# A recurrent-attention layer and a gated feed-forward layer in one kernel: another written-out order, with the loads of w first and unit 4's y transposed by a transfer

## The chip, the cores and the metric

The kernel runs on one core of one Trainium2 chip. The metric is the device time of one execution, in microseconds (us). The core has five engines that each run their own list of instructions in order and wait for each other by semaphores: TensorE (PE in the profile, its weight loads PEld) for matmuls, VectorE (DVE), ScalarE (ACT) and GpSimd (POOL) for elementwise work, and SyncE (SP), which only issues transfers. Transfers (DMA) are issued here from SP and from POOL.

## The reference

The first half is a linear attention with a decaying state, for each batch and head, over 768 tokens with head dimension 48. The second half multiplies two projections of its output and projects the product twice.

```python
def _attn_ref(r, k, v, w, u):
    B, H, S, D = r.shape                     # 4, 8, 768, 48
    state = np.zeros((B, H, D, D))
    for t in range(S):
        kt, vt, rt, wt = (k[:, :, t], v[:, :, t], r[:, :, t], w[:, :, t])
        cur = np.einsum('bhd,bhe->bhde', u[None] * kt, vt)
        y[:, :, t] = np.einsum('bhd,bhde->bhe', rt, state + cur)
        state = wt[:, :, :, None] * state + np.einsum('bhd,bhe->bhde', kt, vt)

def _moe_ref(x, w1, w2, w3, w_out):          # x: 3072 x 384, d_ff 1024
    a = x @ w1
    b = x @ w2
    h = a * b @ w3
    return h @ w_out
```

## The kernel before, in words

The tokens are cut into six chunks of 128, and the work into 13 units: a unit is one chunk of one or two batches (`UNITS`, line 14; units 0 and 1 are chunk 0 of one batch each, all others have two batches). For each unit t the following steps run; their names are those of the table `ORDER`.

*Loads* (lines 316 to 335): `win_t`, `kin_t`, `rin_t`, `vin_t`. Most are issued from POOL, where a transfer can change float32 to bfloat16. Unit 0's r, k and v come from SP as float32 and are cast by an engine (`rc_0`, `kc_0`, `vc_0`, line 330).

*Attention* (`unit`, from line 388): the logarithm of w (`ln`, line 408), its running sum over the chunk by a matmul with a triangle of ones LT (`cs`, line 424), the exponentials of it (`ne`, `e`), and k and r scaled by them (`KRk`, line 445, and `KRr`). k and r are needed transposed. TensorE does it by matmuls with an identity (`trk`, line 512, `trr`, line 497), with an eviction from PSUM behind (`trke`, line 516, `trre`); for the units in `DMA_K` and `DMA_R` a transposing transfer on SP's queue does it (`dtk`, `dtr`). The units in `RAW` transpose the unscaled r (`trw`, line 465), have the running sum a second time in transposed form (`csT`, line 453, its exponential `et`), and multiply afterwards (`KRw`, line 470). Then the scores of a chunk with itself (`m_t_b`, line 551) are masked in one VectorE step (`msk`, line 570) or, for the pairs in `POOL_MASK`, copied by ScalarE (`mcp`, line 557) and masked in place (`maff`, line 565 on POOL, line 563 on VectorE). y is summed in PSUM from the state (`ys`, line 586) and from the masked scores (`yi_t_b`, line 596); the diagonal term is formed beside (`rk`, `ruk`, `dg`, `dv`, lines 520 to 539), and `yb` (line 614) adds the two. `kv` (line 667, in the wide form of `KV_WIDE` line 660), `T`, `S` and `Sb` carry the state on to the next chunk.

*y transposed*: `yt` (line 633) on TensorE with the eviction `xT` (line 637), or, for the units in `DMA_Y`, two transposing transfers `dty_t_b` (line 623) on SP's queue.

*Feed-forward* (`block`, from line 698): groups `a_t_g` and `b_t_g` of x by w1 and w2 (line 714; two groups a unit in units 0 and 1, four otherwise), a's eviction `asb` (line 719), the product `abT` (line 724), then `o_t_b` (line 730), its eviction `osb` (line 735) and the store `st` (line 740). w3 times w_out is formed once: each of eight row blocks of w3 is transposed (`wt`, line 371, evicted by `w3Te`) and multiplied by w_out (`wm`, line 380, evicted by `w34e`). The weights come in pieces: w1 and w2 in halves (`w1_0`, `w1_1`, `w2_0`, `w2_1`; group g of a unit of two batches needs half 0 for g below 2), w3 in quarters (`w3_0` to `w3_3`), w_out whole (`wo`).

Nothing is scheduled by a program: `ORDER` (line 62) lists all steps with their engines, and each engine runs its steps in the order of that table. `warm7@5` in the table stands for five matmuls on zeros into bank 7 (line 308); they compute nothing that is used. `BANKS` (line 39) names the PSUM bank of each step and, in some keys, the buffer in SBUF (`M`: masked scores, `sa`: evicted a, `so`: output rows). The elementwise buffers of the attention steps exist twice, so unit t + 2 waits until unit t is done with them.

The lines that say where a step runs and when are these two, for the whole kernel:

```python
            name, _, eng = e.partition("@")
            steps[name](eng)
```

Of the kernel before, what the change touches and what calls it, by code (L numbers as in the profile page):

```python
# [56 lines left out]
sa10_2=1 a10_3=2 b10_3=2 sa10_3=0 o10_0=3 so10_0=3 o10_1=5 so10_1=2 cs11=0,1 m11_0=4,5 M11_0=2 m11_1=6,7 M11_1=3
y11=0,1 a11_0=2 b11_0=4 sa11_0=1 a11_1=1 b11_1=7 sa11_1=0 a11_2=6 b11_2=4 sa11_2=0 a11_3=0 b11_3=6 sa11_3=2 o11_0=7
so11_0=0 o11_1=2 so11_1=0 cs12=0,1 m12_0=2,3 M12_0=1 m12_1=4,5 M12_1=0 y12=0,1 a12_0=2 b12_0=1 sa12_0=0 a12_1=7
b12_1=6 sa12_1=2 a12_2=3 b12_2=0 sa12_2=0 a12_3=5 b12_3=4 sa12_3=1 o12_0=4 so12_0=3 o12_1=1 so12_1=1  # L60
# [3 lines left out]
mask1@DVE rin_2@POOL rin_0@SP rc_0@DVE warm0@13 cs_0@PE csT_0@PE ne_0@ACT win_1@POOL I128@POOL vin_2@POOL trw_0@PE  # L64
et_0@ACT kin_0@SP kc_0@DVE rk_0@DVE KRk_0@POOL warm6@5 trk_0@PE ln_2@ACT cs_2@PE pc_0@ACT trke_0@DVE KRw_0@DVE
m_0_0@PE w3_0@POOL u@SP uc@ACT mask@POOL rin_1@POOL vin_0@SP vc_0@ACT kv_0@PE ruk_0@DVE dg_0@DVE dv_0@POOL csT_2@PE
ne_2@ACT KRk_2@DVE trk_2@PE trw_2@PE S_0@DVE msk_0_0@DVE yi_0_0@PE kin_1@POOL rk_2@DVE et_2@ACT trke_2@ACT w1_1@POOL
ruk_2@POOL KRw_2@DVE yb_0@DVE warm5@3 m_2_0@PE m_2_1@PE mcp_2_1@ACT ln_1@ACT msk_2_0@DVE warm4@6 cs_1@PE yi_2_0@PE
dg_2@DVE csT_1@PE pc_1@ACT ne_1@ACT wt_0_0@PE wt_0_1@PE maff_2_1@DVE yt_0@PE xT_0@ACT yi_2_1@PE pc_2@ACT kv_2@PE
et_1@ACT dv_2@DVE KRk_1@DVE wt_1_0@PE trw_1@PE wt_1_1@PE yb_2@DVE yt_2@PE a_0_1@PE KRw_1@DVE trk_1@PE xT_2@ACT  # L70
trke_1@ACT a_2_3@PE S_2@DVE m_1_0@PE w3Te_1@ACT a_2_2@PE w1_0@POOL a_0_0@PE a_2_1@PE w2_1@POOL asb_2_2@ACT vin_1@POOL
# [62 lines left out]
def kernel(  # L134
# [254 lines left out]
    def unit(t):  # L389
# [151 lines left out]
        for b in range(nb):  # L541
# [248 lines left out]
```

## Time and profile before

| | |
|---|---|
| median of 3 executions | 168.65 us (168.05 to 200.98) |
| the profiled execution | 168.6 us, of it the span of the core's instructions 166.9 us |
| granted TensorE clock, mean | 0.990 |
| busy: PE / DVE / POOL / ACT | 154.8 / 129.7 / 106.7 / 96.9 us |
| matmuls on zeros (line 308) | 9.5 us |
| bytes moved | 25.63 MB, mean 154 GB/s |

The span runs from the first to the last instruction of the core; the time of the execution is 1.7 us longer. A busy share says how full an engine is on average; where the time goes is read from the stretches in which the engine that ends last has gaps. The time to landing of a transfer is counted from its issue, and so holds the wait behind the transfers ahead of it.

### The profile page before, as it was taken

What the parts mean: (1) busy time and instruction counts of PE and PEld (TensorE: products, weight loads), DVE (VectorE), ACT (ScalarE), POOL (GpSimd) and SP (SyncE); (2) the same over time, 40 slices, a digit from 0 to 9 for tenths busy, and PEclk for the clock granted to TensorE, in tenths of its full rate; (3) what the DMA queues carried; (4) which work ended last, traced back from release to release, by engine and by line L of the source; (5) the groups of instructions that cost most, each with busy time, mean ns of one, the idle gap of its engine ahead of it and who ended that gap; (6) DMA issues with size and microseconds to landing.
All of it is one profiled execution on the core that took longest, in us unless ns stands there. A gap on an engine that the chain in (4) does not pass through costs nothing.

```text
span 166.9 us, 4592 instructions
## 1 busy us (share of the span) xinstructions
PE 154.8 (93%) x1912; PEld 118.1 (71%) x1913; DVE 129.7 (78%) x203; ACT 96.9 (58%) x160; POOL 106.7 (64%) x96
## 2 busy tenths in 40 slices
PE   6866979999999999999899899997999999999991
PEld 2336568878677779678697677875779786988750
DVE  7339897667898899989998999898997986463610
ACT  3265456247976749995696768837582634252421
POOL 7987999266555099996939959995908770500000
PEclk9996999999999999999999999999999999999999
DMA  6999999999999959999999999999795999153033
GB/s 113 215 163 180 163 188 195 245 168 245 207 151 180 141 65 235 144 157 240 108 180 195 147 207 157 84 96 172 187 137 97 108 164 164 20 166 116 4 113 125
DMA packets 100789, 25.63 MB, mean 154 GB/s; under 512 B 92928, under 2 KB 98688, under 8 KB 100768
## 3 DMA queue, kind: packets, MB, share of 16 engines
q0 software_dynamic: 76208, 15.57, 106.9%
q1 hardware_dynamic: 24560, 9.77, 27.8%
q8 instruction: 15, 0.25, 0.7%
q14 instruction: 6, 0.05, 0.1%
HBM read 27.98 MB, written 4.72 MB: 196 GB/s over the span
## 4 chain that ended last, share of the span: by engine, by line
PE 74%; DVE 13%; DMA 5%; issue 4%; ACT 3%; POOL 1%; DVEq 0%; ACTq 0%; POOLq 0%
PE banks L714 31%; PE banks L730 16%; PE banks L380 6%; DMA win<-in_w_dram 5%; PE banks L551 4%; DVE Mbf L570 3%; PE banks L596 2%; PE banks L371 2%; PE banks L512 2%; DVE dv L539 2%; PE banks L424 2%; DVE KR L445 2%; PE banks L667 2%; PE banks L633 1%; DVE yb L614 1%
## 5 line engine op out<-in xcount | busy, mean ns | idle before, releaser
L714 PE MATMUL banks<-xT,w_bf 128*128 128x256 bf16 (+1 forms) x624 | 69.6, 264 | 1.7 <-DVE Mbf L570 1.7
L714 PEld LDWEIGHTS <-w_bf 128*128 128x128 bf16 x624 | 55.7, 98 | 9.4 <-issue 2.1
L719 ACT COPY a_sb<-banks 128x512 f32<-128x512 f32 x48 | 27.3, 590 | 25.8 <-PE banks L714 14.0
L724 DVE TENSOR_TENSOR abT<-a_sb,banks 128x512 bf16<-128x512 f32 x48 | 31.8, 681 | 8.6 <-PE banks L714 5.7
L730 PE MATMUL banks<-w,abT 128*128 128x384 bf16 x192 | 34.2, 326 | 0.0
L730 PEld LDWEIGHTS <-abT 128*128 128x128 bf16 x192 | 18.1, 98 | 10.7
L570 DVE TENSOR_TENSOR Mbf<-banks,mask 128x1024 bf16<-128x1024 f32 x14 | 17.1, 1218 | 4.3 <-PE banks L551 4.3
L735 ACT COPY osb<-banks 128x384 f32<-128x384 f32 x19 | 9.0, 480 | 14.1 <-PE banks L730 13.1
L614 DVE TENSOR_TENSOR yb<-banks,dv 128x768 bf16<-128x768 f32 (+1 forms) x13 | 11.6, 890 | 4.4 <-POOL dv L539 2.4
L335 POOL DMA_DIRECT2D win<-in_w_dram x12 | 13.9, 1158 | 1.4 <-POOLq L774 0.8
L408 ACT ACTIVATE lw<-win 128x768 bf16<-128x768 f32 (+1 forms) x13 | 10.4, 802 | 6.9 <-DMA win<-in_w_dram 6.9
L557 ACT CAST Mbf<-banks 128x1024 bf16<-128x1024 f32 x10 | 10.2, 1016 | 5.2 <-PE banks L551 3.7
L441 ACT ACTIVATE NEt<-banks 128x768 bf16<-128x768 f32 (+1 forms) x13 | 9.9, 761 | 4.2 <-PE banks L424 2.5
L565 POOL TENSOR_SCALAR_AFFINE_SELECT Mbf<-Mbf 128x1024 bf16<-128x1024 bf16 x5 | 5.4, 1102 | 10.5 <-ACT Mbf L557 10.5
L380 PE MATMUL banks<-wo_bf,w3T 128*128 128x384 bf16 x64 | 11.7, 326 | 0.0
L530 DVE TENSOR_REDUCE dg<-ruk 128x16 f32<-128x768 bf16 (+1 forms) x13 | 11.5, 885 | 0.1
L335 POOL DMA_DIRECT2D vin<-in_v_dram x8 | 9.1, 1140 | 3.8 <-DMA wo_bf<-in_moe_w_out_dram 3.2
L335 POOL DMA_DIRECT2D kin<-in_k_dram x8 | 9.1, 1142 | 3.0 <-PE banks L380 2.7
L335 POOL DMA_DIRECT2D rin<-in_r_dram x8 | 9.0, 1128 | 2.9 <-DMA w_bf<-in_moe_w_dram 2.2
L308 PE MATMUL banks<-zeros 128*128 128x512 bf16 x26 | 9.5, 525 | 1.5 <-DVE zeros L249 1.3
L486 POOL TENSOR_TENSOR KR<-rw,Et 128x768 bf16<-128x768 bf16 x3 | 4.9, 1639 | 8.5 <-DVE rw L478 5.4
L424 PE MATMUL banks<-lw,LT 128*128 128x384 bf16 x24 | 6.2, 325 | 2.7 <-ACT lw L408 1.8
(102 smaller groups left out, 257.2 us busy)
## 6 DMA issues: line engine op xcount, KB each, us to landing
out_dram<-osb SPq DMA_DIRECT2D x24, 192.0 KB, 2.3
win<-in_w_dram POOLq DMA_DIRECT2D x10, 384.0 KB, 8.6
w_bf<-in_moe_w_dram POOLq DMA_DIRECT2D x4, 512.0 KB, 13.3
w_bf<-in_moe_w_dram POOLq DMA_DIRECT2D x4, 384.0 KB, 6.9
kin<-in_k_dram POOLq DMA_DIRECT2D x7, 192.0 KB, 9.3
rin<-in_r_dram POOLq DMA_DIRECT2D x7, 192.0 KB, 9.5
vin<-in_v_dram POOLq DMA_DIRECT2D x7, 192.0 KB, 7.5
wo_bf<-in_moe_w_out_dram POOLq DMA_DIRECT2D x1, 768.0 KB, 10.6
```

The source lines that it names most:

```text
L335: QUEUE[eng].dma_start(dst, src)
L380: nc.tensor.matmul(one(f"wm{fi}")[:, :DM], lhsT=w3T[fi % 2][:, gi, :], rhs=wo_bf[:, gi, :], start=(gi == 0), stop=(gi == FI - 1))
L408: nc.scalar.activation(LW[:, :, :D], ww, Act.Ln)
L441: nc.scalar.activation(N_.rearrange("t (b h) d -> t b (h d)", b=nb), cs_view(), Act.Exp, scale=-1.0)
L530: nc.vector.reduce_sum(dgs, ruks, axis=AX.X)
L557: copier(eng)(Mbf[bank[f"M{t}_{b}"]], mview())
L570: nc.vector.tensor_mul(Mbf[bank[f"M{t}_{b}"]], mview(), mask.rearrange("s (j q) t -> s j q t", j=2))
L614: nc.vector.tensor_add(ybs.rearrange("t b (q e d) -> t e (b q) d", e=2, d=D), yview().rearrange("t e (x d) -> t e x d", d=D), dvs.rearrang ...
L714: nc.tensor.matmul(o[:, f, :], lhsT=wt[:, di, fi * P:(fi + 1) * P], rhs=x[:, di, :T], start=(di == 0), stop=(di == DI - 1))
L719: copier(eng)(a_sb[bank[f"sa{t}_{g}"]], one(f"a{t}_{g}"))
L724: nc.vector.tensor_mul(ab[:, g * per:(g + 1) * per, :T], sa.rearrange("p (f t) -> p f t", t=T), one(f"b{t}_{g}").rearrange("p (f t) -> p f ...
L730: nc.tensor.matmul(one(f"o{t}_{b}")[:, :DM], lhsT=ab[:, fi, b * C:(b + 1) * C], rhs=w34[:, fi, :], start=(fi == 0), stop=(fi == FI - 1))
```

## The change

Five tables change, no code. `DMA_Y` loses unit 8 and gains unit 4: y of unit 4 is now transposed by two transfers on SP's queue, and y of unit 8 by TensorE. `POOL_MASK` names ten pairs, five of them as before, `KV_WIDE` names units 3 and 4 in place of 1 and 10. `ORDER` and `BANKS` are new throughout; 71 steps change their engine, and every engine's list is in another order. There are 28 matmuls on zeros where the table had 27: 17 ahead of `cs_0` (13 before), then 5, 4 and 2.

```diff
-DMA_Y = {8, 9, 10, 11, 12}
+DMA_Y = {4, 9, 10, 11, 12}
 F32_IN = {0}
-POOL_MASK = {(2, 1), (3, 0), (5, 1), (6, 1), (7, 1), (8, 0), (8, 1), (10, 0), (11, 1), (12, 1)}
+POOL_MASK = {(2, 0), (5, 0), (6, 1), (7, 1), (9, 0), (10, 0), (10, 1), (11, 1), (12, 0), (12, 1)}
 Y_PE = set()
-KV_WIDE = {1, 10}
+KV_WIDE = {3, 4}
...
-table@ACT zeros@DVE padkr@DVE padet@DVE padlw@DVE win_0@POOL ln_0@ACT padr@DVE ones@DVE win_2@POOL kin_2@POOL LT@POOL
...
+table@ACT zeros@DVE kin_0@SP ones@DVE padlw@DVE kc_0@ACT win_0@POOL win_1@POOL padkr@DVE LT@POOL ln_0@ACT warm0@17
...
```

The built programs show what the tables make of it. First POOL's list at the start of the program, where the loads are issued; `win_0_78`, `win_1_79` and `win_2_80` are the w rows of units 0, 1 and 2, and so with kin, rin and vin. Before:

```order
L335 DMA win_0_78<-in_w_dram 128x8x48
L335 DMA win_2_80<-in_w_dram 128x16x48
L335 DMA kin_2_69<-in_k_dram 128x16x48
L259 ISA
L259 AFFINE_SELECT LT_148<-LT_148 128x128
L335 DMA rin_2_64<-in_r_dram 128x16x48
L335 DMA win_1_79<-in_w_dram 128x8x48
L263 AFFINE_SELECT I128_150<-I128_150 128x128
L335 DMA vin_2_74<-in_v_dram 128x16x48
L445 TENSOR_TENSOR KR_0_94<-kin_0_67,NEt_0_90 128x8x48
L361 DMA w3_bf_143<-in_moe_w3_dram 128x2x1024
```

And after:

```order
L335 DMA win_0_78<-in_w_dram 128x8x48
L335 DMA win_1_79<-in_w_dram 128x8x48
L259 ISA
L259 AFFINE_SELECT LT_148<-LT_148 128x128
L335 DMA win_2_80<-in_w_dram 128x16x48
L335 DMA kin_2_69<-in_k_dram 128x16x48
L263 AFFINE_SELECT I128_150<-I128_150 128x128
L335 DMA rin_2_64<-in_r_dram 128x16x48
L361 DMA w3_bf_143<-in_moe_w3_dram 128x2x1024
L335 DMA kin_1_68<-in_k_dram 128x8x48
L335 DMA rin_1_63<-in_r_dram 128x8x48
L335 DMA vin_2_74<-in_v_dram 128x16x48
```

The w rows of unit 1 move ahead of those of unit 2, the first quarter of w3 ahead of the v rows of unit 2, and unit 0's scaled k (`KRk_0`, line 445) leaves POOL. Behind these rows the weights now come as w2_0, w1_1, w2_1, w1_0, then the w rows of unit 3, then w_out; before they came as w1_1, w1_0, w2_1, w2_0, w_out, w rows of unit 3. The v rows of unit 3, which stood behind the last quarter of w3, stand ahead of the w rows of unit 4 and of that quarter.

Second VectorE's list between the masked scores of unit 0 and the first evictions of the feed-forward part; `Mbf_0_98` holds the masked scores of unit 0, and buffers with `_0_` in their name there are used by units 0 and 2, `_1_` by unit 1. Before:

```order
L570 TENSOR_TENSOR Mbf_0_98<-banks_61,mask_149 128x1024
L520 TENSOR_TENSOR rk_0_102<-rin_2_64,kin_2_69 128x768
L470 TENSOR_TENSOR KRT_0_96<-banks_61,ETt_0_92 128x1024
L614 TENSOR_TENSOR yb_0_110<-banks_61,dv_0_108 128x2x4x48
L570 TENSOR_TENSOR Mbf_2_100<-banks_61,mask_149 128x1024
L530 TENSOR_REDUCE dg_0_106<-ruk_0_104 128x16
L563 TENSOR_TENSOR Mbf_1_99<-Mbf_1_99,mask_149 128x1024
L539 TENSOR_TENSOR dv_0_108<-vin_2_74,dg_0_106 128x768
L445 TENSOR_TENSOR KR_1_95<-kin_1_68,NEt_1_91 128x8x48
L614 TENSOR_TENSOR yb_0_110<-banks_61,dv_0_108 128x2x8x48
```

And after:

```order
L570 TENSOR_TENSOR Mbf_0_98<-banks_61,mask_149 128x1024
L470 TENSOR_TENSOR KRT_0_96<-banks_61,ETt_0_92 128x1024
L520 TENSOR_TENSOR rk_0_102<-rin_2_64,kin_2_69 128x768
L445 TENSOR_TENSOR KR_1_95<-kin_1_68,NEt_1_91 128x8x48
L524 TENSOR_TENSOR ruk_0_104<-rk_0_102,u_bc_153 128x768
L530 TENSOR_REDUCE dg_0_106<-ruk_0_104 128x16
L614 TENSOR_TENSOR yb_0_110<-banks_61,dv_0_108 128x2x4x48
L570 TENSOR_TENSOR Mbf_2_100<-banks_61,mask_149 128x1024
L470 TENSOR_TENSOR KRT_1_97<-banks_61,ETt_1_93 128x512
L637 COPY xT_0_122<-banks_61 128x3x128
L614 TENSOR_TENSOR yb_0_110<-banks_61,dv_0_108 128x2x8x48
```

The sum of unit 2's y (the last row of both) now comes behind the eviction of unit 0's transposed y (`xT_0_122`, line 637), which ScalarE did; `ruk_2` comes from POOL, and unit 2's `dv` and the mask of its first scores (`maff_2_0`) go there.

In TensorE's list the feed-forward part opened with a_0_1, behind yt_2; it now opens with b_0_0, ahead of yt_2, with two matmuls on zeros right before it. `cs_1` and `csT_1` stand before unit 2's scores. The casts of unit 0's r and k go from VectorE to ScalarE, where that of r stands behind ln_1 and et_0; the cast of u goes from ScalarE to VectorE, that of v from ScalarE to POOL.

Third SP's list from the first output stores on; `osb` are output rows, `yb_0_110` is y of unit 4. Before:

```order
L740 DMA out_0_dram<-osb_2_139 128x384
L740 DMA out_0_dram<-osb_3_140 128x384
L335 DMA win_1_79<-in_w_dram 128x16x48
L740 DMA out_0_dram<-osb_2_139 128x384
L491 DMA_TRANSPOSE KRT_1_97<-KR_1_95 128x8x128
```

And after:

```order
L740 DMA out_0_dram<-osb_0_137 128x384
L740 DMA out_0_dram<-osb_2_139 128x384
L623 DMA_TRANSPOSE xT_0_122<-yb_0_110 128x3x128 x2
L491 DMA_TRANSPOSE KRT_1_97<-KR_1_95 128x8x128
L740 DMA out_0_dram<-osb_3_140 128x384
```

The two transposing transfers of unit 4 stand behind two stores and ahead of the transposed r of unit 7 (line 491); the w rows of unit 9 have left this queue for POOL's.

More of the change, by code (lines that the diff above doesn't have):

```diff
@@ L57 @@
[L57 to L60, printed above, removed]
+wt0=4 wm0=5 wt1=7 wm1=1 wt2=6 wm2=7 wt3=2 wm3=0 wt4=1 wm4=3 wt5=7 wm5=7 wt6=6 wm6=0 wt7=3 wm7=3 cs0=3 ct0=4 tr0=1
@@ L61 @@
 """
 ORDER = """
-table@ACT zeros@DVE padkr@DVE padet@DVE padlw@DVE win_0@POOL ln_0@ACT padr@DVE ones@DVE win_2@POOL kin_2@POOL LT@POOL
[L64 to L71, printed above, removed]
-b_2_3@PE w3Te_0@DVE msk_1_0@DVE rk_1@POOL yi_1_0@PE a_2_0@PE ruk_1@DVE dg_1@DVE dv_1@DVE Sb_2@DVE asb_2_3@ACT
@@ new lines @@
+KRk_0@DVE trw_0@PE w2_0@POOL trk_0@PE ln_2@ACT cs_2@PE KRw_0@DVE dg_0@DVE vin_0@SP pc_1@ACT pc_0@ACT trke_0@DVE
+vc_0@POOL kv_0@PE S_0@DVE ne_2@ACT KRk_2@DVE m_0_0@PE csT_2@PE et_2@ACT w1_1@POOL mask@POOL trk_2@PE dv_0@POOL
+msk_0_0@DVE trke_2@ACT trw_2@PE vin_1@POOL cs_1@PE ne_1@ACT KRw_2@DVE warm6@4 m_2_0@PE wt_1_0@PE pc_2@ACT w2_1@POOL
+wt_1_1@PE mcp_2_0@ACT rk_2@DVE w3Te_1@ACT w1_0@POOL yi_0_0@PE m_2_1@PE KRk_1@DVE trk_1@PE trke_1@ACT ruk_2@DVE
+dg_2@DVE yb_0@DVE kv_2@PE trw_1@PE msk_2_1@DVE wt_0_0@PE wt_0_1@PE maff_2_0@POOL yi_2_0@PE yt_0@PE KRw_1@DVE yi_2_1@PE
```

155 lines of the change are left out of this document (81 added, 74 removed).

## The prediction

> **What bounds the kernel now.** I read the busy time by stretch first, to see which engine is full and where it isn't. The columns are the stretch in us, then for PE, PEld, DVE, ACT and POOL the busy time and the number of instructions, then the granted TensorE clock, the DMA share and GB/s.
>
> ```profile
> 0.00:23.90 23.90, 18.13 (x174) 10.54 (x176) 16.54 (x36) 10.29 (x18) 21.27 (x27) 0.93 1.37 170
> 23.90:31.00 7.10, 6.89 (x96) 5.95 (x94) 5.28 (x10) 4.45 (x7) 5.91 (x7) 1.00 1.39 210
> 31.00:80.00 49.00, 49.00 (x705) 38.47 (x703) 43.05 (x69) 35.41 (x58) 32.84 (x28) 1.00 1.93 178
> 80.00:90.00 10.00, 9.28 (x93) 7.65 (x91) 9.08 (x13) 7.69 (x13) 7.09 (x7) 1.00 1.66 173
> 90.00:110.00 20.00, 19.45 (x299) 15.31 (x298) 19.47 (x29) 14.12 (x23) 17.85 (x13) 1.00 1.53 143
> 110.00:120.00 10.00, 8.89 (x100) 6.55 (x99) 8.98 (x11) 6.37 (x10) 8.10 (x8) 1.00 1.07 162
> 120.00:163.30 43.30, 43.18 (x460) 33.59 (x457) 27.28 (x41) 18.11 (x32) 13.63 (x12) 1.00 0.69 110
> ...
> sum 166.90, PE 154.81 PEld 118.05 DVE 129.69 ACT 96.89 POOL 106.68; mean PE 19.35 PEld 14.76 DVE 16.21 ACT 12.11 POOL 13.33
> ```
>
> From 23.9 us to its last matmul at 163.3 TensorE is busy but for 0.21 + 0.72 + 0.55 + 1.11 + 0.12 = 2.7 us. So the time is: when the dense work starts, plus that work, plus a tail of 166.9 - 163.3 = 3.6 us. The page's cost groups say what of the busy time is filler, the matmuls on zeros that keep the array running:
>
> ```profile
> L308 PE MATMUL banks<-zeros 128*128 128x512 bf16 x26 | 9.5, 525 | 1.5 <-DVE zeros L249 1.3
> ```
>
> Useful matmul time is 154.81 - 9.5 = 145.3 us, and the change keeps it: it trades y's transposes of unit 4 for those of unit 8 (same count), and the wide form of kv in units 1 and 10 for units 3 and 4. So what can be won is in the opening, where 23.9 us pass before the first matmuls of the feed-forward part (line 714), and in the 2.7 us of later idle. Third, I read the chain of waits through the opening (start us, us, what):
>
> ```profile
> 2.40 7.85 DMA win<-in_w_dram
> ...
> 10.33 0.84 ACT lw L408
> ...
> 11.24 0.40 ACT u_bc L304
> ...
> 12.79 1.23 DVE KR L445
> ...
> 14.07 1.03 PE banks L512 x8
> ...
> 16.50 1.06 PE banks L308 x2
> 17.55 0.57 PE banks L551 x16
> ...
> 22.39 0.96 DVE yb L614
> ...
> 23.39 0.51 PE banks L633 x6
> 23.90 0.67 PE banks L714 x12
> ...
> 25.60 0.35 PE banks L551 x8
> ...
> 40.05 0.45 PE banks L371 x8
> 40.50 0.45 PE banks L512 x8
> ```
>
> Everything hangs on unit 2: its w rows land at 10.25, its scores (m_2) start at 17.55, its y is added at 22.39 and transposed, and only then does the dense work begin, since a_0_1 stands behind yt_2 in TensorE's order.
>
> **The opening, step by step.** Loads: the w rows of unit 2 are now the third transfer of the GpSimd queue, behind those of units 0 and 1 and the making of LT.
>
> ```profile
> 1.34 2.24 POOL L335 DMA_DIRECT2D win<-in_w_dram  x2 [0.83 <-POOLq L774]
> ...
> 4.78 0.33 POOL L259 TENSOR_SCALAR_AFFINE_SELECT LT<-LT 128x128 bf16<-128x128 bf16 x1
> ```
>
> Two issues and LT take 1.34 + 2.24 + 0.33 = 3.91, against 2.40 now, and with the same 7.85 us to landing w arrives at 11.76, 1.5 us later. From landing to m_2_0 now takes 17.55 - 10.25 = 7.30 us. Out of this path go the cast of u on ScalarE (0.40) and the two matmuls on zeros (1.06) that stand right before m_2_0. The four zeros that replace them come earlier, while TensorE would wait for the eviction of unit 2's k. That gives 11.76 + 7.30 - 1.46 = 17.6. The long end keeps all of it: 19.06. The short end is a full clock for the two sets of eight transposes, of which one took 1.03 here against 0.45 later: 17.6 - 1.0, so 16.6 (the second set priced alike). I take 17.6, because the removals are rows of the chain and the clock is not known.
>
> From m_2 to the dense work: the first group is now b_0_0, which needs y of unit 0 only (and the first half of w2, issued among the first weights), and unit 2's y may come later. What lies ahead of it on VectorE after m_2 is, by like instructions, ruk_2, dg_2, yb_0, the mask of m_2_1, KRw_1 and xT_0:
>
> ```profile
> 16.68 0.55 DVE L614 TENSOR_TENSOR yb<-banks,dv 128x384 bf16<-128x384 f32 x1
> 17.93 1.23 DVE L570 TENSOR_TENSOR Mbf<-banks,mask 128x1024 bf16<-128x1024 f32 x1 [0.70 <-PE banks L551]
> 19.07 0.94 DVE L530 TENSOR_REDUCE dg<-ruk 128x16 f32<-128x768 bf16 x1
> ...
> 23.26 0.41 DVE L470 TENSOR_TENSOR KRT<-banks,ETt 128x512 bf16<-128x512 bf16 x1
> ...
> 30.79 0.36 DVE L637 COPY xT<-banks 128x384 bf16<-128x384 bf16 x1 [0.44 <-PE banks L633]
> ...
> 46.61 0.55 DVE L524 TENSOR_TENSOR ruk<-rk,u_bc 128x768 bf16<-128x768 bf16 x1
> ```
>
> Their sum is 0.55 + 0.94 + 0.55 + 1.23 + 0.41 + 0.36 = 4.04; with m_2's 0.57 ahead, xT_0 is ready at 17.6 + 0.57 + 4.04 = 22.2. TensorE's m_1_0 fits beside xT_0, and two matmuls on zeros follow (9.5 / 26 = 0.37 each): b_0_0 starts at 22.9.
>
> To compare, I count to a point where both kernels have done the same: all groups of units 0 to 2, cs_3, the first two products of w3 with w_out and the transposes of four w3 blocks. Now that is reached at 40.05 + 0.45 = 40.50, after 16.6 us with 0.21 idle, so 16.39 of work. The changed order does yt_2 (0.51) inside this stretch and has done m_1_0 (0.35) and trk_1 (half of a 0.45, 0.22) before it: 16.33. Started at 22.9 it ends at 39.2, a gain of 1.3 us. With m_2_0 at its short and long ends the gain is 2.3 and -0.2.
>
> It holds only if the weights keep up. The third piece of w3 (w3_2) is the tightest that I found:
>
> ```profile
> 27.19 0.74 POOL L361 DMA_DIRECT2D w_bf<-in_moe_w_dram  x1
> ```
>
> ```profile
> w_bf<-in_moe_w_dram POOLq DMA_DIRECT2D x1, 512.0 KB, 14.4
> ```
>
> ```profile
> 43.25 0.55 PE banks L371 x8
> ```
>
> Issued at 27.19, landed 14.4 us later at 41.6, used at 43.25: 1.65 us of cover. The same bytes stand ahead of it after the change, and GpSimd's queue issues the first four weight pieces without rk_1 and ruk_2 between them, so I don't let it land later; the cover is just enough for 1.3.
>
> **Unit 4's y.** Its six transposes and one eviction leave TensorE and ScalarE, two transposing transfers come onto SP's queue. The queue holds them behind two output stores, and dtr_7 behind them. The price is nothing if they land before a_4_0.
>
> ```profile
> L623 SPq DMA_TRANSPOSE xT<-yb x10: 1178/1240/1257, 108.6 to 146.4; - x10
> ```
>
> ```profile
> xT<-yb SPq DMA_TRANSPOSE x10, 2.5
> ```
>
> ```profile
> vin<-in_v_dram POOLq DMA_DIRECT2D x1, 192.0 KB, 13.2
> ```
>
> ```profile
> 58.15 2.71 PE banks L730 x16
> ...
> 61.18 1.31 PE banks L714 x12
> ```
>
> Between yi_4_1 and a_4_0 TensorE now has six groups of unit 3 (3 x 1.31), three outputs (1.5 x 2.71) and five sets of eight transposes or like (5 x 0.45): 10.2 us without its smaller steps. VectorE has five elementwise steps (0.55 each) and yb_4 (0.96) first: 3.7; the first issue takes 1.24 and the second transfer lands 2.5 after its own: 7.4 in all, 2.8 spare. The transfers of this row all lie after 108 us, with lighter loads. The nearest row for the loaded queue is the v load issued between 36 and 40 us, 13.2 to landing. I take 2.5, because that row has the same kind of transfer; the other end is a rival below.
>
> **The rest.** Steps of the later units change engines in both directions and masks change their form (14 on VectorE alone before and after); their waits are unknown. Bounds: the 0.72 + 0.55 + 1.11 = 2.4 us of idle between 80 and 120 us may vanish or double. I take no change. The last steps are again outputs of unit 12, an eviction and a store: the tail stays 3.6. The profiled execution took 168.6 us, 1.7 over its span, and the median is 168.65, so no correction is needed: 168.6 - 1.3 = 167.3 us.
>
> A row on contention belongs here:
>
> ```profile
> L539 DVE TENSOR_TENSOR dv<-vin,dg x5: 558/948/2395, 20.5 to 79.0; 128x768 bf16<-128x768 bf16 x4, 128x384 bf16<-128x384 bf16 x1
> ```
>
> The longest of these is dv_6, at 79.0, with GpSimd at work on KRk_7; it took 1.45 more than the median, and the idle 0.72 between 80 and 90 us came behind it. The change swaps the two engines of this pair and leaves GpSimd fewer elementwise steps. The Trainium skill (SBUF — State Buffer, Who interferes with whom) says that a VectorE instruction with two SBUF inputs contends with a GpSimd one that reads SBUF; by that the 0.72 goes, and the sum would be 166.6. I leave it out of the sum, because the row shows one such place and the new order makes others.
>
> **The rivals.**
> *Both gains at once (faster).* The opening at its short end, 2.3, and no idle from 80 to 120, 2.4: 168.6 - 4.7 = 163.9. For it: the idle places all lie where VectorE is busy 9.0 to 9.7 of 10, and dv_6, the longest step there, leaves VectorE. Against: as many steps move onto VectorE as off it, so it has no room to give.
> *The transfers bind.* TensorE reaches w3_2, w3_3 and unit 4's loads earlier, but v of unit 3 now goes ahead of the last piece of w3, and the loads land when they did: the gain is used up waiting, 168.6. For it: 1.65 of cover is little. Against: the bytes are the same.
> *The opening gets longer (slower).* Unit 0's casts move to ScalarE, r's behind ln_1 and et_0, so all of unit 0's products start later; w of unit 2 is 1.5 later. With m_2_0 at 19.06 the dense work starts 1.5 later than I say. If the array's clock is low there too, the products between 17 and 22 us (some 2 us of them at full clock, an estimate from x8 at 0.45 and m_2 at 0.57) take twice as long, 2 more: 167.3 + 3.5 = 170.8. For it: x8 transposes took 1.03 at 14.07, and 9 zeros now stand between cs_0 and the dense work's start where 14 stood (two more come at its edge). Against: TensorE's own steps are packed closer there. It decides from m_2_0 later than about 18.9. The Trainium skill (TensorE: Matmul & The Clock Gate, Part 1) says the array runs at half rate after an idle window of some 3.4 us until as long a busy one has passed; the row at 14.07 agrees in kind, though TensorE was not idle that long at a stretch. By that rule alone, with the idle no longer than now, the sum would stay 167.3.
> *y of unit 4 lands late (slower).* At 13.2 to landing it comes 3.7 + 1.24 + 13.2 = 18.1 after yi_4_1, against 10.2 of counted and up to 4 of uncounted work: 4 to 8 us of wait, 167.3 + 4 = 171.3 at its near end. It decides from a landing later than about 5.3 us.
> That the change doesn't do what it says is excluded by the built order.
>
> **Chances and range.** Forecast 0.50 (own range 166.2 to 168.4); both gains 0.13; transfers bind 0.14; longer opening 0.12; late y_4 0.06; other new waits in the middle, up to the doubled 2.4 (169.7), 0.05. What a measurement can tell here from no change is about 2%, 3.4 us: below 165.3 or above 172.0. Faster takes most of the both-gains case: 0.13 with the forecast's lower tail. Slower takes the far half of the two slower rivals and of the rest: 0.12. Same: 0.75. The range 164.6 to 171.0 takes in the forecast, the bound transfers, most of the longer opening and the near part of the fast case.
>
> **What would show it.** Right: the first matmul of line 714 at 22.9 (21.9 to 24.4), m_2 at about 17.6, no idle before the w3 transposes (line 371) between 39 and 46 us, transfers of y_4 landing within 5 us, TensorE idle 2 to 3 us from 31 us on. Wrong: a start past 24.2, idle at line 371 or 714 behind a transfer, or more than 4 us of new idle in the middle.

## The result, and the profile after

The changed kernel takes 170.12 us (median of 20 runs, 168.24 to 172.77), the kernel before 168.37 us (20 runs beside them): 1.0078 times as long, 95% interval 1.0051 to 1.0105. I had forecast 167.3 us and a small gain. The time lies in the range, and the change is within the 2% that I called no change, but the sign is wrong, and the interval shows that it is. The runs of the changed kernel differ among themselves by 2.7% (the twelve with a mean TensorE clock of 0.98 or less all took more than 169.3 us), and since a ratio leaves out every run more than 1.5% above the fastest of its kernel, the median over all runs stands beside it.

The profiled execution took 170.14 us, its span 168.4. Busy time by stretch, columns as in the prediction:

```profile
0.00:23.90 23.90, 19.81 (x213) 11.94 (x215) 15.06 (x38) 12.83 (x21) 22.03 (x29) 1.00 1.45 177
31.00:80.00 49.00, 49.00 (x676) 38.10 (x675) 42.70 (x64) 35.63 (x62) 36.85 (x30) 1.00 2.04 177
80.00:90.00 10.00, 9.86 (x147) 7.70 (x146) 8.88 (x15) 7.76 (x13) 8.29 (x7) 1.00 1.66 186
90.00:110.00 20.00, 18.80 (x226) 14.92 (x225) 18.43 (x27) 12.97 (x26) 11.04 (x10) 1.00 1.81 160
110.00:120.00 10.00, 8.66 (x130) 6.21 (x127) 9.97 (x15) 6.50 (x12) 4.53 (x3) 1.00 0.96 111
120.00:164.80 44.80, 42.90 (x440) 32.76 (x432) 30.39 (x40) 17.89 (x31) 12.12 (x9) 0.96 0.56 102
...
sum 168.40, PE 156.14 PEld 117.98 DVE 130.67 ACT 97.60 POOL 101.46; mean PE 19.52 PEld 14.75 DVE 16.33 ACT 12.20 POOL 12.68
```

The opening is shorter: TensorE works 19.81 of the first 23.9 us against 18.13, and from 31 to 80 us it does not stop. What was won there is lost behind 80 us. TensorE's idle from 80 us on is 0.14 + 1.20 + 1.34 + 1.90 = 4.6 us, against 2.5, and the last long stretch has a granted clock of 0.96 instead of 1.00. The clock makes the same work longer. The matmuls on zeros, to be taken off, are now:

```profile
L308 PE MATMUL banks<-zeros 128*128 128x512 bf16 x26 | 9.1, 510 | 1.5 <-DVE zeros L249 1.3
```

Without the zeros the matmuls take 156.1 - 9.1 = 147.0 us, 1.7 more than before, though they are the same matmuls but for the form of kv in four units.

The largest loss lies at 126 us. The first fence is VectorE's timeline there, the second GpSimd's, the third TensorE's (start us, busy us, line and operation, idle before and what ended it):

```profile
125.18 0.94 DVE L530 TENSOR_REDUCE dg<-ruk 128x16 f32<-128x768 bf16 x1
126.16 4.08 DVE L539 TENSOR_TENSOR dv<-wo_bf,dg 128x768 bf16<-128x768 bf16 x1
130.16 0.68 DVE L724 TENSOR_TENSOR abT<-a_sb,banks 128x512 bf16<-128x512 f32 x1
130.76 0.94 DVE L614 TENSOR_TENSOR yb<-banks,dv 128x768 bf16<-128x768 f32 x1
```

```profile
126.18 1.65 POOL L520 TENSOR_TENSOR rk<-rin,kin 128x768 bf16<-128x768 bf16 x1
127.78 1.64 POOL L520 TENSOR_TENSOR rk<-w_bf 128x768 bf16<-128x768 bf16 x1
129.50 2.25 POOL L524 TENSOR_TENSOR ruk<-rk,u_bc 128x768 bf16<-128x768 bf16 x1
```

```profile
128.69 1.46 PE L730 MATMUL banks<-w,abT 128*128 128x384 bf16 x8
131.76 0.40 PE L551 MATMUL banks<-KRT 64*128 64x128 bf16 x8 [1.60 <-DVE yb L614]
132.35 0.40 PE L551 MATMUL banks<-KRT 64*128 64x128 bf16 x8 [0.20 <-DVE abT L724]
```

dv_10 takes 4.08 us instead of 0.95 while GpSimd does rk_12, rk_11 and ruk_11 (lines 520 and 524) at its usual 1.65 and 1.64; ruk_11 is then 0.6 longer than the 1.65 it took before. Behind dv_10 stand abT of unit 9 and y of unit 10, and TensorE's next product, m_11_0, may not start before y of unit 10 has been read, since the new table of banks gives m11_0 the banks 0 and 1 that y10 holds. So TensorE waits 1.60 us. The bank table has a part in this wait, then, and no run here changes it alone. The same happens, shorter, at 114 us: rk_10 on VectorE beside rw_11 on GpSimd, and the out projection behind them waits 1.33.

```profile
114.17 2.35 DVE L520 TENSOR_TENSOR rk<-w_bf 128x768 bf16<-128x768 bf16 x1
114.44 1.65 POOL L478 TENSOR_TENSOR rw<-w_bf,iw 128x768 bf16<-128x768 bf16 x1
117.91 1.46 PE L730 MATMUL banks<-w,abT 128*128 128x384 bf16 x8 [1.33 <-DVE yb L614]
```

And after the idle at 130 us the clock falls, here by single microseconds:

```profile
130.00:131.00 1.00, 0.16 (x1) 0.09 (x1) 1.00 (x3) 0.07 (x1) 1.00 (x1) 1.00 1.70 151
131.00:132.00 1.00, 0.24 (x8) 0.24 (x8) 1.00 (x2) 0.51 (x1) 1.00 (x2) 1.00 1.31 243
132.00:133.00 1.00, 0.81 (x17) 0.54 (x12) 1.00 (x3) 0.21 (x1) 0.90 (x1) 1.00 0.04 8
133.00:134.00 1.00, 1.00 (x7) 0.61 (x6) 1.00 (x2) 0.80 (x1) 0.00 (x0) 0.63 0.61 100
134.00:135.00 1.00, 1.00 (x4) 0.44 (x3) 1.00 (x3) 0.00 (x0) 0.00 (x0) 0.50 1.68 83
135.00:136.00 1.00, 1.00 (x5) 0.46 (x4) 1.00 (x2) 0.00 (x0) 0.00 (x0) 0.50 2.03 159
136.00:137.00 1.00, 1.00 (x6) 0.53 (x5) 0.97 (x2) 0.48 (x1) 0.00 (x0) 0.66 0.80 50
```

Half the clock for 0.37/0.5 + 2 + 0.34/0.5 = 3.4 us costs 1.7 us of work.

Such long steps are not new. Among VectorE's products of two SBUF tensors of 128x768 from 31 us on, the kernel before has four above 1.1 us (2.40 at 79.0, 1.20 at 83.0, 1.59 at 98.4, 2.62 at 110.8), the changed one four as well (1.22 at 88.1, 1.32 at 96.4, 2.35 at 114.2, 4.08 at 126.2). Over their usual 0.55 and 0.95 that is 5.2 us lost before and 6.4 after: it is less the number of collisions that changed than where they stand and what waits behind them.

The account against before: the opening gives 40.50 - 37.71 = 2.8 us at the comparison point (worked out in the section on why), the idle takes 2.1 back and the clock 1.7. That leaves +1.0, and the span grew by 1.5; the other 0.5 I did not place.

### The profile page after: what moved, and what is told of

It reads as the page before. It is cut to its first block, busy times and chain, and to the rows that moved or that the text cites. A ratio compares the mean times of both kernels' runs of the same rounds, so it can differ in the third digit from the quotient of the medians.

```text
span 168.4 us, 4579 instructions
## 1 busy us (share of the span) xinstructions
PE 156.1 (93%) x1908; PEld 118.0 (70%) x1910; DVE 130.7 (78%) x204; ACT 97.6 (58%) x164; POOL 101.5 (60%) x92
## 4 chain that ended last, share of the span: by engine, by line
PE 69%; DMA 10%; DVE 7%; issue 5%; POOL 5%; ACT 1%; SPq 0%; POOLq 0%; DVEq 0%
PE banks L714 30%; PE banks L730 16%; PE banks L380 6%; DMA vin<-in_v_dram 5%; DMA KRT<-KR 5%; PE banks L551 3%; PE banks L596 2%; PE banks L371 2%; DVE abT L724 2%; PE banks L424 2%; PE banks L667 2%; POOL win L335 2%; PE banks L512 1%; PE banks L633 1%; PE banks L586 1%
## 5 line engine op out<-in xcount | busy, mean ns | idle before, releaser
L714 PEld LDWEIGHTS <-w_bf 128*128 128x128 bf16 x624 | 55.1, 98 | 7.9 <-issue 0.7
L730 PE MATMUL banks<-w,abT 128*128 128x384 bf16 x192 | 36.0, 337 | 1.3 <-DVE yb L614 1.3
L730 PEld LDWEIGHTS <-abT 128*128 128x128 bf16 x192 | 18.7, 100 | 13.3 <-issue 3.1
L565 POOL TENSOR_SCALAR_AFFINE_SELECT Mbf<-Mbf 128x1024 bf16<-128x1024 bf16 x6 | 6.9, 1145 | 16.7 <-ACT Mbf L557 15.8
L335 POOL DMA_DIRECT2D win<-in_w_dram x13 | 14.9, 1154 | 0.8 <-POOLq L774 0.8
L551 PE MATMUL banks<-KRT 64*128 64x128 bf16 x192 | 8.5, 217 | 2.9 <-DVE yb L614 1.6
L551 PEld LDWEIGHTS <-KRT 64*128 64x128 bf16 x192 | 5.7, 94 | 6.4 <-issue 4.4
```

Of the source, the lines that this page charges most:

```text
L335: QUEUE[eng].dma_start(dst, src)
L551: nc.tensor.matmul(o[:, e, q, :], lhsT=KRTs[a:a + PAD, 0, b * HP + q, :], rhs=KRTs[a:a + PAD, 1, b * HP + q, :], start=True, stop=True)
L714: nc.tensor.matmul(o[:, f, :], lhsT=wt[:, di, fi * P:(fi + 1) * P], rhs=x[:, di, :T], start=(di == 0), stop=(di == DI - 1))
L730: nc.tensor.matmul(one(f"o{t}_{b}")[:, :DM], lhsT=ab[:, fi, b * C:(b + 1) * C], rhs=w34[:, fi, :], start=(fi == 0), stop=(fi == FI - 1))
```

## Experiments

**My theory**: VectorE's steps that read two tensors from SBUF are held up by GpSimd's elementwise steps, the new order put them side by side at two places, and TensorE's clock falls after the longer of the two waits that follow. **The first rival**: TensorE would have waited for data in any case (transposed K and R, loads, y of unit 4), and the long VectorE steps only fill that wait. All kernels were timed beside the kernel before. TensorE's idle time by stretch is read from the same view as above (length of the stretch less the busy time):

| kernel | median us | ratio to before, 95% interval | idle 80-120 us | idle 120-140 us | clock 130-140 us |
|---|---|---|---|---|---|
| before | 168.4 to 168.7 | 1 | 2.38 | 0 | 1.00 |
| changed | 170.12 | 1.0078, 1.0051 to 1.0105 | 2.68 | 1.80 | 0.83 |
| rk_12, rk_11, ruk_11 off GpSimd | 168.54 | 1.0005, 0.9974 to 1.0036 | 3.02 | 0.94 | 1.00 |
| rw_11 off GpSimd | 168.57 | 0.9992, 0.9950 to 1.0033 | 0.55 | 1.79 | 0.83 |
| both | 166.76 | 0.9909, 0.9879 to 0.9940 | 1.60 | 0.94 | 1.00 |
| o_8_0 twice | 168.68 | 1.0037, 1.0001 to 1.0073 | 1.88 | 0.49 | 1.00 |
| y of unit 4 by TensorE | 169.94 | 1.0008, 0.9971 to 1.0046 | 2.55 | 1.79 | 0.83 |
| before, two products more on GpSimd | 176.63 | 1.0464, 1.0427 to 1.0502 | 2.38 | 6.37 | 0.83 |
| both, m_9 later | 167.18 | 0.9925, 0.9898 to 0.9952 | 1.65 | 0.94 | 1.00 |
| the same, rk_11 early | 165.90 | 0.9857, 0.9815 to 0.9899 | 1.66 | 0 | 1.00 |

The differences given below are between medians over all runs. By the ratios, the first four edits in the order of the table are 1.2, 1.45, 2.85 and 0.7 us faster than the changed kernel, and the interval of the fourth overlaps the changed kernel's. A third measure leaves out the opening, which differs from trace to trace: from the start of the out projection o_6_0 (109.69 us in the changed kernel's trace) to the end of the span it is 58.7 us in the changed kernel and 56.1, 57.4, 54.8 and 57.1 in the four, that is 2.6, 1.3, 3.9 and 1.6 less.

### One collision taken away, then the other, then both

```diff
-... rk_12@POOL ... rk_11@POOL ruk_11@POOL dg_11@DVE
+... rk_12@DVE ... rk_11@DVE ruk_11@DVE dg_11@DVE
```

> The changed kernel with three steps of VectorE's kind, rk_12, rk_11 and ruk_11, taken from GpSimd to VectorE at the same places of the list. Collision theory (in the changed kernel's trace dv_10 on VectorE took 4.08 us, not 0.95, while these three ran on GpSimd, and TensorE stood idle 1.60 + 0.20 us behind it and then ran 130-140 us at a granted clock of 0.83): dv_10 takes 0.95 us again, the 1.8 us of idle go, VectorE gets 3 x 0.55 = 1.65 us more work, a part of which may show; with the clock back the span falls by 1.8 + up to 1.7 us: 167 us, 166.5 to 168.5, ratio to the kernel before about 0.995. Late-data theory (TensorE would have waited for the transposed K and R or the loads in any case, the long dv_10 only filled the wait): the idle moves to another releaser and the time stays at 170.1, within 0.5 us.

Measured 168.54 us, 1.6 less than the changed kernel, and just past the long end (168.5) of what the collision theory gave. The clock is back, but 0.94 us of idle stay, for y of unit 11 behind VectorE's longer row. Only the three engine tags differ.

```diff
-cs_12@PE e_12@ACT rw_11@POOL yb_9@DVE
+cs_12@PE e_12@ACT rw_11@DVE yb_9@DVE
```

> The changed kernel with rw_11 alone taken from GpSimd to VectorE. Collision theory: rk_10 on VectorE, 2.35 us beside it in the changed kernel's trace, takes 0.55 us; yb_9 comes 1.3 us sooner and the 1.33 us of TensorE idle before the out projection at 117.9 us go; dv_10 keeps its 4 us unless the steps shift against each other. Time 170.1 - 1.3 = 168.8, 168.3 to 169.8, ratio about 1.002. Late-data theory: no change within 0.4 us, 169.7 to 170.5.

Measured 168.57 us, again 1.55 less. The idle from 110 to 120 us is gone (1.34 to 0), and dv_10, left as it was, still costs 1.79 us and the clock.

> Both edits at once: none of rk_12, rk_11, ruk_11, rw_11 on GpSimd. Collision theory: the gains add up, 3.1 us of idle and up to 1.7 us of lost clock: 165.5 to 167.5 us, ratio 0.985 to 0.995, so faster than both kernels, with the opening's gain of about 2.5 us kept. Late-data theory: 170 us within 0.6. Where VectorE becomes the bound instead (2.2 us more work on it from 110 to 140 us): 168 to 169.5.

Measured 166.76 us: 3.4 less than the changed kernel, about 1.6 + 1.55 added up (in the traces 2.6 + 1.3 = 3.9), and 0.9% faster than the kernel before. The late-data theory said 170 and falls. dv steps of the later units in this kernel, by the view of the tile:

```profile
L539 DVE TENSOR_TENSOR dv<-wo_bf,dg x3: 947/958/958, 105.1 to 136.5; 128x768 bf16<-128x768 bf16 x3
```

The longest is 958 ns, where it was 4,082. VectorE took over four steps at 0.55 us from GpSimd, 2.2 us, and lost the two long steps, 3.13 + 1.80 = 4.9 us: giving these steps to GpSimd had saved VectorE nothing.

### The clock by itself

```diff
-b_9_3@PE o_8_0@PE dty_10_0@SP
+b_9_3@PE o_8_0@PE o_8_0@PE dty_10_0@SP
```

> The changed kernel with the out projection of unit 8's first row issued twice (8 matmuls of 128x384 more, the same result written again), which fills 1.3 us of the 1.6 us in which TensorE stood idle at 130.2 us; dv_10 stays as long as it was. Clock theory (the granted clock falls to 0.83 after that idle because TensorE stood still): the clock of 130 to 140 us is back near 1.0 and the time falls by 1 to 1.7 us, 168.4 to 169.1, though more work is done. If the clock there has another cause: 130 to 140 us stay at about 0.83 and the time stays at 170.1, or rises by up to 0.3 us.

Measured 168.68 us, 1.4 less than the changed kernel with 1.3 us of matmuls more; by the ratios it is 0.7, not clear of noise, so the traces have to carry this part. dv_10 was as long as before, and y of unit 10 as late; only TensorE's idle was filled (its timeline, then the busy time of the stretch):

```profile
129.79 2.76 PE L730 MATMUL banks<-w,abT 128*128 128x384 bf16 x16
132.86 0.40 PE L551 MATMUL banks<-KRT 64*128 64x128 bf16 x8 [0.30 <-DVE yb L614]
133.45 0.40 PE L551 MATMUL banks<-KRT 64*128 64x128 bf16 x8 [0.19 <-DVE abT L724]
133.78 0.83 PE L714 MATMUL banks<-xT,w_bf 128*128 128x256 bf16 x6
134.45 2.76 PE L730 MATMUL banks<-w,abT 128*128 128x384 bf16 x16
```

```profile
130.00:140.00 10.00, 9.51 (x126) 5.99 (x124) 9.78 (x13) 3.47 (x5) 3.92 (x3) 1.00 1.08 121
```

The 16 matmuls of line 730 at 134.45 us take 2.76 us at the full clock; in the kernel with rw_11 off GpSimd, where the clock fell as in the changed one, they take 4.44:

```profile
132.45 4.44 PE L730 MATMUL banks<-w,abT 128*128 128x384 bf16 x16
```

The fall of the clock stands in the three traces with 1.8 us of idle at this place (the changed kernel, rw_11 off GpSimd, y of unit 4 by TensorE) and in none of those with 0.94 us or less. So it comes from TensorE standing still there, and it costs about as much as the wait itself: filling the idle gained 1.6 us behind o_6_0.

### The headline part: y of unit 4

```diff
-DMA_Y = {4, 9, 10, 11, 12}
+DMA_Y = {9, 10, 11, 12}
-yb_4@DVE dty_4_1@SP dty_4_0@SP
+yb_4@DVE ... yt_4@PE ... xT_4@ACT
```

> The changed kernel with its headline part undone: y of unit 4 goes through TensorE (12 matmuls of 128x128 more, 0.34 us) and ScalarE (one copy of 0.82 us) as it did in the kernel before, and its two transposing transfers fall away. Collision theory (the loss has nothing to do with y of unit 4): the two collisions late in the kernel stay, the time is 0.0 to 0.4 us above the changed kernel's, ratio 1.007 to 1.011. Late-data theory (the two transfers of y of unit 4 hold up the queue of transfers and with it what lands later): 1 us or more faster than the changed kernel, ratio 1.002 or less.

The ratio, 1.0008, would speak for the late-data theory and the median, 169.94, against it. I go by the trace (its execution took 170.73 us): both places of waiting stand in it unchanged (1.33 us from 110 to 120, 1.79 from 130 to 140, clock 0.83), and the idle of the other stretches from 31 us on is the changed kernel's within 0.15 us. So the transfers of unit 4 cause neither of the two waits. Whether they cost anything elsewhere, up to the 1.2 us between the two ratios, these runs do not tell.

### The collision alone, put into the kernel before

```diff
-kin_12@POOL m_10_1@PE
+kin_12@POOL rw_11@POOL rw_11@POOL m_10_1@PE
```

> The kernel BEFORE the change, with one thing added: GpSimd writes rw of unit 11 twice more (the same values), 2 x 1.64 us, in a stretch in which it stood idle, from about 122 us, while VectorE has rk_11 and dv_10, both with two inputs in SBUF, to do. Collision theory: one of these steps takes 3 to 4.5 us instead of 0.55 or 0.95, what follows on VectorE comes some 3.3 us later, of which 1.21 us are VectorE's idle time before abT at 127.7 us; TensorE gets an idle stretch of 0.5 to 2 us there and the time rises by 0.5 to 3 us (more where the clock falls): ratio 1.003 to 1.018. Rival (VectorE's long steps in the changed kernel waited for something else, GpSimd beside them is chance): rk_11 and dv_10 stay at 0.55 and 0.95 us and the time within 0.3 us.

Measured 176.63 us: 8 us more, far over the 3 that I gave at most. VectorE's and GpSimd's timelines, then TensorE's two waits:

```profile
122.52 1.99 DVE L520 TENSOR_TENSOR rk<-w_bf 128x768 bf16<-128x768 bf16 x1
124.43 2.39 DVE L539 TENSOR_TENSOR dv<-wo_bf,dg 128x768 bf16<-128x768 bf16 x1
...
128.22 5.16 DVE L486 TENSOR_TENSOR KR<-rw,Et 128x768 bf16<-128x768 bf16 x1
```

```profile
122.41 3.59 POOL L478 TENSOR_TENSOR rw<-w_bf,iw 128x768 bf16<-128x768 bf16 x2 [0.87 <-DVE KR L486]
...
128.94 1.65 POOL L524 TENSOR_TENSOR ruk<-rk,u_bc 128x768 bf16<-128x768 bf16 x1
130.55 0.83 POOL L689 TENSOR_TENSOR Sbf<-Tst,pc 128x384 bf16<-128x384 f32 x1
131.33 1.62 POOL L520 TENSOR_TENSOR rk<-rin,kin 128x768 bf16<-128x768 bf16 x1
```

```profile
127.59 2.78 PE L714 MATMUL banks<-xT,w_bf 128*128 128x256 bf16 x24 [2.37 <-DVE abT L724]
...
134.57 0.37 PE L596 MATMUL banks<-wo_bf,Mbf 128*128 128x48 bf16 x8 [4.00 <-DVE Mbf L570]
```

The two products held up rk_11 and dv_10 by 1.44 + 1.44 us: together what I expected, but spread over two steps, where I had one of them take 3 to 4.5 us. What I had not seen is what follows: VectorE, now 3 us late, reaches KRr_12 when GpSimd starts its row of ruk_11, the state and rk_12, and that one step lasts 5.16 us, until that row is over. In the kernel before, VectorE passes this place in time. One collision made the next. KRr_12 starts 0.72 us ahead of ruk_11, long enough for its usual 0.55, while GpSimd is issuing a load; what held it in that time is open. The kernel before has the same at 110.8 us: a step begun while GpSimd issues a load takes 2.62 us and ends 0.4 us behind the first GpSimd step that follows the load.

### What of GpSimd's work does it

The same place in the kernel before, with copies (one tensor read) and with memsets (nothing read) of a dead buffer in place of the products:

```diff
-kin_12@POOL m_10_1@PE
+kin_12@POOL copy@POOL copy@POOL copy@POOL m_10_1@PE
```

> The kernel BEFORE the change with three copies of r of unit 11 into the dead buffer of rw of unit 11 on GpSimd, at the place where the two extra products stood that made rk_11, dv_10 and KRr_12 long and the time 176.6 us. A copy reads one tensor in SBUF, the product two. If any step of GpSimd that reads SBUF holds up VectorE's steps with two inputs in SBUF: rk_11 and dv_10 together take the length of the copies longer, time 170 to 177 us. If only GpSimd's two-input steps do: rk_11 0.55, dv_10 0.95 us, time 168.6 within 0.5.

Measured 169.54 us, ratio 1.0068 (1.0043 to 1.0093), under the 170 that I gave for any step that reads: the two steps are 1.25 us longer together, not by the 3.48 us of the copies. With five memsets instead:

> The same place in the kernel BEFORE, with five memsets of the dead buffer of rw of unit 11 on GpSimd, which read nothing. If it is GpSimd's reading that holds VectorE up: rk_11 0.55 and dv_10 0.95 us, time 168.6 within 0.5 us. If any work of GpSimd on SBUF does, or the shift of GpSimd's later steps by some us is enough: rk_11 or dv_10 over 1.5 us, or the time 170 us or more.

Measured 168.74 us, ratio 1.0024 (1.0000 to 1.0047). GpSimd's and VectorE's timelines, first with the copies, then with the memsets (the added code moves dv from line 539 to 544):

```profile
122.02 3.48 POOL L531 COPY rw<-w_bf 128x768 bf16<-128x768 bf16 x3 [0.86 <-DVE KR L486]
122.14 1.18 DVE L520 TENSOR_TENSOR rk<-w_bf 128x768 bf16<-128x768 bf16 x1
123.24 1.57 DVE L544 TENSOR_TENSOR dv<-wo_bf,dg 128x768 bf16<-128x768 bf16 x1
```

```profile
122.40 4.07 POOL L531 MEMSET rw<- 128x768 bf16 x5 [0.69 <-DVE KR L486]
122.53 0.55 DVE L520 TENSOR_TENSOR rk<-w_bf 128x768 bf16<-128x768 bf16 x1
123.00 0.95 DVE L544 TENSOR_TENSOR dv<-wo_bf,dg 128x768 bf16<-128x768 bf16 x1
```

Beside 4.07 us of memsets the two steps keep their 0.55 and 0.95 us; beside copies each is 0.6 longer; beside products each is 1.44 longer. So it is GpSimd's reading of SBUF that holds VectorE up, and longer steps hold it longer. Of the two steps each is delayed by less than one GpSimd step beside it takes (1.64 us a product, 3.48 / 3 = 1.16 a copy). That reading counts and writing does not agrees with the Trainium skill (SBUF — State Buffer, Who interferes with whom), by which a VectorE instruction with two SBUF inputs contends with a GpSimd one that reads SBUF, not with one that only writes.

### Unit 9's late transfer, and VectorE's row before y of unit 11

In the changed kernel TensorE also waits 0.79 us at 107 us for a transposing transfer of unit 9. With both collisions gone it waited 1.05. The wait is not in every trace: with rw_11 off GpSimd and with o_8_0 twice, whose order up to there is the same, TensorE did not wait for it, and idle from 90 to 110 us was 0.55.

```diff
-b_7_3@PE m_9_1@PE ... m_9_0@PE b_7_2@PE ... yt_8@PE ... b_7_0@PE
+b_7_3@PE ... b_7_2@PE ... yt_8@PE ... b_7_0@PE m_9_1@PE m_9_0@PE
```

> The kernel with both groups of steps off GpSimd, and in addition the K R products of unit 9 (m_9_1, m_9_0) moved behind b_7_2, the transposes of y of unit 8 and b_7_0 on TensorE, that is 1.66 us of work later. In the trace of the kernel without this move the transposing transfer of unit 9's K landed 7.64 us after its issue and TensorE stood idle 1.05 us for it at 108.4 us. If that late landing is on the path that sets the end: 0.7 to 1.2 us faster than without the move, 165.5 to 166.1 us, ratio about 0.985. If VectorE's row of steps behind it is what counts (the products come later, so do mask and y of unit 9): no change, 166.4 to 167.1.

Measured 167.18 us, no gain over 166.76. The trace tells why, and I had not looked: cs_11 now stands right behind m_9_0 and writes the same banks 2 and 3, so TensorE waits for ScalarE's copy of m_9_0 instead.

```profile
110.11 0.48 PE L424 MATMUL banks<-lw,LT 128*128 128x384 bf16 x2 [1.11 <-ACT Mbf L557]
```

Next, VectorE's row at 131 to 138 us, behind which TensorE still stood idle 0.94 us:

```diff
-abT_9_3@DVE m_11_0@PE ... rk_12@DVE ... rk_11@DVE ruk_11@DVE ... ruk_12@DVE
+abT_9_3@DVE rk_11@DVE m_11_0@PE ... ruk_11@DVE ... rk_12@DVE ruk_12@DVE
```

> The kernel with m_9 later, and on VectorE rk_11 moved ahead of the mask of unit 11, into 0.78 us in which VectorE stood idle at 130.7 us, and rk_12 behind y of unit 11. In the trace without this, y of unit 11 came at 137.6 us at the end of an unbroken row of VectorE steps, and TensorE stood idle 0.94 us for it. If VectorE's row is what bounds there: y of unit 11 comes 0.9 us sooner and the time falls by 0.5 to 0.9 us against the kernel without this, ratio about 0.980. If TensorE finds a later wait instead: no change within 0.3 us.

Measured 165.90 us, 1.3 less than without it. From 120 to 140 us TensorE has no idle left. This is the fastest kernel of the study: 0.9857 (0.9815 to 0.9899) of the kernel before.

> The last kernel (both groups off GpSimd, m_9 later, rk_11 early) with the running sum of unit 11 (cs_11) moved behind the out projection o_6_0 on TensorE, 1.3 us later. In the traces with m_9 later TensorE no longer waits for the transposed K of unit 9, but 1.11 us for ScalarE's copy of m_9_0 out of the two banks that cs_11, right behind it, writes: the wait had only moved. If that wait is on the path: 0.7 to 1.1 us faster than the kernel without this, 164.8 to 165.3 us, ratio about 0.979. If another wait takes its place again: within 0.3 us of 165.9.

Here cs_11 goes behind o_6_0. The wait of 1.11 us is gone from the trace, three smaller ones (0.29, 0.16 and, behind the transposed y of a unit, 0.36 us) stand in it instead, and the time is not better: 166.2 us is the median of five of the six times (164.91 to 167.68; the sixth, 538 us, I leave out), ratio 0.9864 (0.9818 to 0.9910). The difference from the kernel without it is within what six runs can tell. Whether unit 9's transfer is worth anything stays open.

### The opening's order of weights

```diff
-vin_2 w2_0 w1_1 ... b_0_0@PE ... a_0_1@PE
+vin_2 w1_1 w2_0 ... a_0_1@PE ... b_0_0@PE
```

> The kernel with rk_11 early (both groups off GpSimd, m_9 later), with one part of the change's opening undone: the first half of w1 is loaded ahead of the first half of w2 again, and the first group of the dense work is a_0_1, as in the kernel before, instead of b_0_0. If the opening's gain comes from this order of the weights: the dense work's first group starts about 1 us later (24 us and more) and the time is 1 us longer, about 166.9. If it comes from the order of the w rows and of the first steps, which stay: the first group starts between 21.5 and 23.3 us as in the eight traces with the new opening, and the time stays at 165.9 within 0.6 us.

Measured 166.07 us (0.9842, 0.9810 to 0.9874), the same as the 165.90 without it. The first group starts at 23.69 us, 0.4 past the 23.3 that I gave; the trace without it has 23.24. So w2 ahead of w1 is not where the opening's gain comes from.

## Why the prediction was wrong, point by point

- **What bounds the kernel** (start, dense work, tail): right, and the tail is 168.4 - 164.8 = 3.6 us as forecast. That the useful matmul time stays at 145.3 us was wrong, 147.0, because I took the clock of the dense work as given.
- **The opening, gain 1.3 (2.3 to -0.2)**: right in mechanism and sign, too small. In the changed kernel's trace m_2 starts at 16.57 (forecast 17.6, short end 16.6) and the first matmul of line 714 at 21.47 (22.9):

```profile
16.57 0.40 PE L551 MATMUL banks<-KRT 64*128 64x128 bf16 x8
...
21.47 0.83 PE L714 MATMUL banks<-xT,w_bf 128*128 128x128 bf16 x12
```

  The comparison point, the end of the four w3 blocks' transposes, is reached at 38.16, and by then this order has done one set of eight (0.45) more than I counted: 37.71, against 40.50 before and 39.2 forecast. The chain of waits there:

```profile
37.94 0.22 PE banks L371 x4
38.16 0.45 PE banks L465 x8
```

  That is the early end of a spread. In nine traces with this opening m_2 starts between 16.6 and 18.5, mean 17.4, the dense work between 21.5 and 23.3, mean 22.3, and the point lies between 37.7 and 39.6, mean 38.7; in four with the old opening the point lies between 40.5 and 40.9, mean 40.7. So the gain is 2.0 us on average. The start of m_2 was well taken; the mis-sized terms are the way from it to the dense work (4.9 us, forecast 5.3, since VectorE's six steps overlap at their ends and take 3.8, not 4.04) and the single trace of before (40.5, at the early end). The rival of half clock in a longer opening did not come: the clock from 12 to 20 us was granted between 0.57 and 1.00 from trace to trace, and even at 0.57 the dense work starts at 23.2, earlier than before.
- **The loads**: right. No idle stands before line 371 or 714 from 31 to 80 us (49.00 of 49.00 busy). It is not so in every execution: in the trace with o_8_0 twice TensorE stops there for 0.47 us, at 53 us, behind the late landing of a load of w rows.
- **y of unit 4**: hidden, as forecast, but not by my number. The row of SP's timeline and, from the view of transfers between 61.5 and 64 us, the landing:

```profile
62.08 2.77 SPq L623 DMA_TRANSPOSE xT<-yb  x2
```

```profile
xT<-yb SPq DMA_TRANSPOSE x2, 7.6
```

  They land after 7.6 us, not 2.5: the row from the lightly loaded end of the kernel was the wrong one. a_4_0 does not wait because the smaller steps that I had not counted lie ahead of it as well, and y of unit 4 undone moved neither of the two large waits. I said that it decides from 5.3; that was too early.
- **"The rest ... I take no change"**: this is the step that failed. Its bounds, 0 to 4.8 us of idle between 80 and 120 us, held (2.68), and it was the wrong stretch: the largest new wait lies at 130 us, where the kernel before had none, and the clock's 1.7 us that follow a wait were in no term at all. Together the middle and late part cost about 170.12 - 168.37 + 2.0 = 3.75 us. That the time still lies in the stated range is luck: the room above 169.7 was left for a longer opening, which did not come, and the opening, 0.7 us better than forecast, took a part of the loss away.
- **The row on contention**: I had the cause in my hand. I wrote that the order swaps one such pair (dv_6 and KRk_7) and "makes others", and left it there. In the new order that pair no longer overlaps (KRk_7 on VectorE at 74.9 us takes 0.55, dv_6 on GpSimd at 77.5 takes 1.47), and the idle between 80 and 90 us fell from 0.72 to 0.14. That agrees with the Trainium skill's rule there (SBUF — State Buffer, Who interferes with whom), though no run changes this pair alone. The others could have been looked for in the built order, which does not show by itself that they overlap in time: dv_10 on VectorE with rk_12, rk_11 and ruk_11 in a row on GpSimd, rk_10 beside rw_11. Two collisions of the size of the row that I quoted (1.45 us each), on stretches where VectorE is 9 to 10 of 10 busy, would have made the sum 167.3 - 0.6 + 2.9 = 169.6 us.
- **The rivals**: "other new waits in the middle", 0.05, up to 169.7, is what came, a little past its 169.7, and it got the smallest chance. Late y of unit 4, bound transfers and a longer opening did not come. That what would show me wrong was "more than 4 us of new idle in the middle" set the mark too high: 2.1 us of new idle and the clock were enough.

What stays open: 0.5 us of the account; why the changed kernel's times spread over 2.7% (one execution of it was traced); what unit 9's transfer costs; what the new bank table costs.

## What to carry to other kernels

Where a scheduler moves elementwise steps between VectorE and GpSimd, list for the new order which VectorE steps that read two tensors from SBUF can fall beside GpSimd steps that read SBUF, and price each pair by the length of the GpSimd step, not by VectorE's own. A step on GpSimd that takes three times as long as on VectorE (1.64 against 0.55 us) relieves nothing when it stands beside such work; four tags changed back turned a loss of 0.8% into a gain of 0.9%. Where TensorE's idle is gathered in one place, the clock's fall can cost as much again as the wait (1.7 us behind 1.8).

## What I had not expected of the hardware

- A VectorE step can be passed over by several GpSimd steps in a row: dv_10 (0.95 us) took 4.08 us and ended 0.8 us behind the second of two of them, KRr_12 (0.55 us) took 5.16 us and ended 0.4 us behind the third of three.
- 1.8 us of idle between 130.1 and 132.4 us was followed, from 133.3 us on, by 3.4 us at half the clock. 1.1 us (at 114 us in the kernel before), 1.3 (at 118 us in the changed one), 0.5 (with o_8_0 twice) and even 2.4 in a row (at 125 us, with two products more in the kernel before) did not; 4.0 us behind them did. So the length of the idle alone does not decide, and what does is open. The Trainium skill (TensorE: Matmul & The Clock Gate, Part 1) has the clock fall after an idle window of about 3.4 us: the length of the slow stretch agrees with that window, the idle in front of it was half as long.
- Transposing transfers issued while the GpSimd queue's loads are under way landed 7.6 us after their issue (unit 4's y), against 2.5 behind 108 us.
